# An FFN output gate: from the finished down sums (VectorE) into the down weights (GpSimd)

## Chip, cores and metric

The kernel runs on one NeuronCore of a Trainium2 chip. The metric is the device time of one execution in microseconds (us). The kernel before was run three times: 493.52, 494.44 and 493.52 us, median 493.52.

## What is computed

An adaptive-LayerNorm block over 2048 tokens of width 448, all in float32. A conditioning vector gives six rows of 448 (shift, scale and gate, for each of two sublayers). The second sublayer is a SwiGLU feed-forward network (FFN) of hidden width 1792, whose output is multiplied by its gate row `gb` before it is added to the residual:

```python
mod = (_silu(c) @ w_mod).reshape(c.shape[0], 6, 1, -1)
sa, ca, ga, sb, cb, gb = (mod[:, 0], mod[:, 1], mod[:, 2], mod[:, 3], mod[:, 4], mod[:, 5])
h = _layernorm(x, axis=-1) * (1 + ca) + sa
x = x + ga * _A_ref(h, ...)            # state-space convolution over the tokens
h = _layernorm(x, axis=-1) * (1 + cb) + sb
x = x + gb * ((_silu(h @ w_gate) * (h @ w_up)) @ w_down)
```

`gb` has one number for each of the 448 output columns, the same for all tokens. So `gb * (p @ w_down)` is also `p @ (w_down * gb)`, with the row multiplied into every row of `w_down`.

## The kernel before

**Tiling.** The tokens are 16 tiles of 128, taken in six blocks of 2, 2, 3, 3, 3, 3 tiles (`BLOCKS`). The hidden width is 14 steps of 128 (`NF`). For each block, `ffn` runs the 14 steps. In step f, `gate_up(f, nw)` makes both products of the block's tokens with weight tile f in two PSUM banks (L686), ScalarE takes the silu of one (L701), VectorE multiplies the other by it (L714). Then `down(f - 1)` adds the hidden part of the step before to the block's output sums, one PSUM bank `DN[q]` for each token tile (L730).

**Splits.** Matmuls run on a rounded type. To keep float32 precision each operand is split in a high part (a rounding copy) and a low part (the difference), and a product takes three matmuls: high by high, high by low, low by high. The hidden part is split by ScalarE (`phi`, L717) and VectorE (`plo`, L718). The weights are split once, in block 0: `split_w` for gate and up (ScalarE L120, VectorE L122 and L124) and `split_d` for down (ScalarE cast L112, VectorE subtraction L114). The split weights stay in SBUF for the later blocks.

**Order.** Nothing is scheduled for the kernel: instructions stand on each engine's queue in the order in which the code issues them. Ahead of the FFN the start-up works through a list of names (`PLAN`); in it `d00`, `d01`, `d10`, `d11` are the ScalarE and VectorE halves of the splits of down tiles 0 and 1. `eg` copies the finished row `gb` from PSUM to SBUF (L421), near the end of that list. The splits of down tiles 2 to 13 are at the head of `gate_up(f)` of block 0, that is ahead of that step's silu and product on the same engines.

**Loads.** SP's queue loads the weights. Raw down tiles rotate through three SBUF buffers (`rawd`): the load of tile f + 3 (L107) is issued in step f and waits until tile f has been split; it stands behind the load of gate-up tile f + 5 (L102), which waits for the split of tile f + 2.

**Other work in the steps.** `TIMES` places the norms and the convolution of the next block's tiles in the steps of this one (VectorE L148 to L186, L824 to L877; GpSimd L165 to L172 for the root of the variance; from block 1 on also GpSimd L824, L830, L843). `transposes` at the last step brings the next block's normalised rows into the layout `hhi`, `hlo` (TensorE L206, ScalarE L207 and L209, VectorE L211 and L212).

**End of a block.** For each token tile VectorE multiplies the down sum by `gb` into a spare SBUF buffer (L757), adds it to the residual `x` (L758), and SP stores the tile (L759). In the last block, tile 1's add is GpSimd's, and the last tile goes in two column parts, 256 and 192 wide (L753, L754), the first stored from ScalarE's queue and the second from SP's (L755).

Of the kernel before, what the change touches and what calls it, by code (L numbers as in the profile page):

```python
# [12 lines left out]
OP = mybir.AluOpType  # L13
# [3 lines left out]
L, D, N, F = 2048, 448, 256, 1792  # L17
# [4 lines left out]
NF = F // 128  # L22
# [18 lines left out]
ORDER = """sf x0 x1 sc m10 se m11 sd m20 m21 m00 sb m01 sa m40 m41 d0 w0 m30 m31 m50 w2 d1 x2 w1 x3 d2 m51"""  # L41

PLAN = """t1 t4 pa0 t2 pa1 pg0 pg1 t3 S1 ca h00 S2 ps0 wr wi ps1 a2 m0 t5 a3 sq1 k0 cb0 S3 ga cb1 w0 h01 gd h11 m1 k1 gm0 h10
hd0 sb0 gm1 hd1 gc1 v00 v10 gc0 o00 o01 sq0 o02 o10 v01 sa w02 d10 o13 st0 r0 o12 cbr v11 d11 o11 o14 sb1 n10 w2 w01
st1 r1 d00 sbr e0 n11 n20 du0 tr0 n21 hi0 du1 tr1 l0 fs l1 sbt lo00 hi1 w1 lo10 fl lo01 sbc x1 e1 lo11 w11 w21 x0 eg
w22 lc cbt w12 d01 cbc"""
EPS = 1e-5


# [3 lines left out]
def f32(ap):  # L53
    return ap.bitcast(F32)
# [3 lines left out]
def tile_kernel(ctx, tc, x, a_re, a_im, b_re, b_im, c_re, c_im, log_dt, dskip,  # L58
                wd, wgate_up, states, groups, vecs, dft, idft, out):
    nc = tc.nc  # L60
    sy, ve, sc, po, pe = nc.sync, nc.vector, nc.scalar, nc.gpsimd, nc.tensor
# [28 lines left out]
    wgu, raw, wdn, wp = {}, {}, {}, {}  # L90
# [5 lines left out]
    xn_of = [spare[2][:, 0:512], spare[2][:, 512:1024], spare[0][:, 0:512]]  # L96
# [9 lines left out]
        wp[j] = [pool.tile([128, D], F32R, name=f"wd{q}{j}") for q in "hl"]  # L106
        sy.dma_start(wdn[j], wd[j * 128:(j + 1) * 128, :])  # L107

    def split_d(j, part=None):
        hi, lo = wp[j]  # L110
        if not part:
            sc.copy(hi, wdn[j])  # L112
        if part != 0:
            ve.tensor_tensor(lo, wdn[j], f32(hi), op=OP.subtract)  # L114

    def split_w(j, part=None, en=ve):
        hi, lo, st = wgu[j][:, :, 0:3, :], wgu[j][:, :, 4:7, :], wgu[j][:, :, 3, :]
        w = raw[j]
        if not part:
            sc.copy(wgu[j][:, :, 0:4, :], w)  # L120
        if part is None or part == 1:
            en.tensor_tensor(lo, w[:, :, 0:3, :], f32(hi), op=OP.subtract)  # L122
        if part is None or part == 2:
            en.tensor_tensor(st[64:128], w[64:128, :, 3, :], f32(st[64:128]), op=OP.subtract)  # L124
# [16 lines left out]
    sbc = const.tile([128, 4], F32)  # L141
# [102 lines left out]
    with tc.tile_pool(name="pre", bufs=1) as pre:  # L244
# [54 lines left out]
        for z in range(2):  # L299
            e = slice(64 * z, 64 * z + 64)  # L300
# [110 lines left out]
        def flag_of():  # L411
# [10 lines left out]
        do = lambda g, *a: (lambda: g(*a))  # L422
# [35 lines left out]
            "w0": do(split_w, 0, 0), "w01": do(split_w, 0, 1, WV), "w02": do(split_w, 0, 2, WV),  # L458
            "w1": do(split_w, 1, 0), "w11": do(split_w, 1, 1), "w12": do(split_w, 1, 2),
            "w2": do(split_w, 2, 0), "w21": do(split_w, 2, 1), "w22": do(split_w, 2, 2),  # L460
            **{f"d{j}{z}": do(split_d, j, z) for j in range(2) for z in range(2)},
            "sq0": do(square, 0), "sq1": do(square, 1), "fs": flag_sum, "fl": flag_of,
        }
        names = PLAN.split()
# [197 lines left out]
    def run_blocks(pools, stages, first=None):  # L662
        work, hid = pools.work, pools.hid
        def ffn(ts, fresh, last, todo):
            n = len(ts) * 128
            dn, pp = [], {}
            qz = [(q, z) for z in range(3) for q in range(len(ts))]

            def gate_up(f, nw):
                head = fresh and f == 0  # L670
                if fresh and f > 1:
                    split_d(f)
                w = wgu[f]
                p = hid.tile([128, 256], F32, name="p") if fresh else p_of[f % 2]
                hi = hid.tile([128, MB * 128], F32R, name="phi")
                lo = hid.tile([128, MB * 128], F32R, name="plo")
# [39 lines left out]
                    split_w(nw, 1)  # L716
                sc.copy(hi[:, 0:n], ps[1][:, 0:n])  # L717
                ve.tensor_tensor(lo[:, 0:n], ps[1][:, 0:n], f32(hi[:, 0:n]), op=OP.subtract)  # L718
                if nw is not None:
                    split_w(nw, 2)  # L720

            def down(f, qz):
                if not dn:
                    dn.extend(DN[q] for q in range(len(ts)))
                hi, lo = pp[f]
                wh, wl = wp[f]
                for q, z in qz:
                    cs = slice(q * 128, (q + 1) * 128)
                    u, v = ((hi, wh), (hi, wl), (lo, wh))[z]
                    pe.matmul(dn[q][:, 0:D], u[:, cs], v, start=f == 0 and z == 0, stop=f == NF - 1 and z == 2)  # L730
# [12 lines left out]
                down(NF - 1, qz)  # L743
            m = len(ts) - 1
            for q, i in enumerate(ts):
                t = xn_of[q][:, 0:D]
                if last:
                    down(NF - 2, [(e, z) for e in ((0, 1) if q == 0 else range(q + 1, min(q + 2, m + 1))) for z in range(3)])
                    down(NF - 1, [(q, z) for z in range(3)])

                if last and q == m:
                    for a, e, dma in ((0, 256, sc), (256, D, sy)):
                        ve.tensor_tensor(dn[q][:, a:e], dn[q][:, a:e], gb[:, a:e], op=OP.mult)  # L753
                        ve.tensor_tensor(xs[i][:, a:e], dn[q][:, a:e], xs[i][:, a:e], op=OP.add)  # L754
                        dma.dma_start(out[i * 128:(i + 1) * 128, a:e], xs[i][:, a:e])  # L755
                    continue
                ve.tensor_tensor(t, dn[q][:, 0:D], gb, op=OP.mult)  # L757
                (po if last and q else ve).tensor_tensor(xs[i], xs[i], t, op=OP.add)  # L758
                sy.dma_start(out[i * 128:(i + 1) * 128, :], xs[i])  # L759

        for j in range(NP0, NP0 + NS):
            pools.load(j)
# [10 lines left out]
        for b, ts in enumerate(TILES):  # L773
            todo = {}
            if b + 1 < len(TILES):
# [208 lines left out]
```

## Time and profile before

| what | value |
|---|---|
| time of the three runs, median | 493.52 us (493.52 to 494.44) |
| profiled execution, span from first to last instruction | 491.7 us |
| mean granted TensorE clock in it | 0.995 |
| start-up until the first FFN matmul | 39.1 us |
| block 0 (L686, L730), to the first matmul of block 1 | 39.1 to 98.9 us |
| end of the last matmul | 484.06 us |
| last store issued | 486.32 us |
| splits of the down weights | 14 casts on ScalarE, median 570 ns; 14 subtractions on VectorE, median 624 ns |
| gate's multiplies on the down sums | 15 of 448 columns (median 616 ns), 2 parts of 256 and 192 |

The profile is of one further execution, whose own time is its span; the difference of 1.8 us to the runs' median lies outside its first and last instruction. In its rows, PE is TensorE, PEld its weight loads, DVE VectorE, ACT ScalarE, POOL GpSimd and SP SyncE; a q behind an engine is its instruction queue, where DMAs are issued. A timeline row is: start, length, engine, line, operation, written tile <- read tiles, shape, and in brackets the idle time ahead of it with what ended it. A row of one line's instructions gives the least, median and longest duration in ns. A row of a table by stretches gives, behind the length of the stretch, the busy time (and count) of PE, PEld, DVE, ACT and POOL, then granted clock, DMA share and GB/s. A row of DMA issues gives count, size and median us from issue to landing. In the chain of waits a row is start, length, and what the end of the program was waiting for then.

### The profile page before, as it was taken

The numbers are of one execution on the slowest core, as the hardware profiler recorded it, in microseconds if no ns is written. First come the engines' busy times: TensorE is split into PE (matmuls) and PEld (weight loads), VectorE is DVE, ScalarE is ACT, GpSimd is POOL, SyncE is SP. The second block draws the span as 40 slices with busy tenths as digits, with TensorE's granted clock in tenths as the row PEclk, the third lists the DMA queues.
The fourth block names the chain that finished last, engine by engine and source line by source line (L and its number), as shares of the span: only waits on it lengthen the run. The fifth ranks groups of instructions, "written<-read, shape, count | busy, mean of one in ns | idle before, by whom it ended". The sixth has DMA issues, their size and how long they took to land.

```text
span 491.7 us, 6939 instructions
## 1 busy us (share of the span) xinstructions
PE 482.0 (98%) x2759; PEld 452.5 (92%) x2759; DVE 265.9 (54%) x516; ACT 161.3 (33%) x348; POOL 70.3 (14%) x92
## 2 busy tenths in 40 slices
PE   8999999999999999999999999999999999999993
PEld 5659988999999999999999999999999999999992
DVE  4868999568886445634735553473465353221113
ACT  5665555622226112224412222521222161111110
POOL 2241001000010032411006140101541100000000
PEclk9999999999999999999999999999999999999998
DMA  8944752020000200000300000030000001000001
GB/s 309 404 165 159 232 188 86 15 95 1 0 3 21 75 1 0 2 1 2 98 15 1 2 0 2 2 112 1 0 2 1 1 0 57 0 1 0 1 0 64
DMA packets 11979, 26.04 MB, mean 53 GB/s; under 512 B 1825, under 2 KB 7842, under 8 KB 11938
## 3 DMA queue, kind: packets, MB, share of 16 engines
q1 hardware_dynamic: 11232, 25.33, 14.9%
q8 instruction: 23, 0.38, 0.3%
q10 hardware_dynamic: 706, 0.18, 0.2%
q14 instruction: 18, 0.15, 0.1%
HBM read 21.80 MB, written 3.67 MB: 52 GB/s over the span
## 4 chain that ended last, share of the span: by engine, by line
PE 97%; DVE 1%; ACT 0%; issue 0%; POOL 0%; POOLq 0%; DVEq 0%
PE bank L686 58%; PE dn L730 27%; PE bank L225 2%; PE bank L241 1%; PE bank L206 1%; PE dn L420 1%; PE bank L229 1%; PE cv L851 0%; PE cv L849 0%; PE bank L850 0%; PE cv L225 0%; PE bank L376 0%; PE bank L863 0%; PE cv L206 0%; PE cv L864 0%; PE dn L310 0%
## 5 line engine op out<-in xcount | busy, mean ns | idle before, releaser
L686 PE MATMUL bank<-hhi,gu 128*128 128x384 f32 (+1 forms) x1169 | 210.2, 319 | 0.0
L686 PEld LDWEIGHTS bank<-hhi,gu 128*128 128x128 f32 x1169 | 190.4, 188 | 3.1 <-issue 0.7
L686 PE MATMUL bank<-hlo,gu 128*128 128x384 f32 (+1 forms) x668 | 131.6, 319 | 0.0
L714 DVE TENSOR_TENSOR bank<-raw,bank 128x384 f32<-128x384 f32 (+1 forms) x69 | 36.9, 534 | 144.0 <-PE bank L686 128.6
L686 PEld LDWEIGHTS bank<-hlo,gu 128*128 128x128 f32 x668 | 109.7, 188 | 0.1
L717 ACT CAST phi<-bank 128x384 fp32r<-128x384 f32 (+1 forms) x83 | 36.8, 444 | 145.2 <-DVE bank L714 145.2
L701 ACT ACTIVATE raw<-bank 128x384 f32<-128x384 f32 (+1 forms) x70 | 32.8, 469 | 121.8 <-PE bank L686 115.4
L718 DVE TENSOR_TENSOR plo<-bank,phi 128x384 fp32r<-128x384 f32 (+1 forms) x83 | 42.5, 512 | 37.5 <-ACT phi L717 37.5
L730 PE MATMUL dn<-wdh,phi 128*128 128x448 f32 x224 | 60.4, 368 | 0.0
L730 PE MATMUL dn<-wdh,plo 128*128 128x448 f32 x224 | 60.2, 367 | 0.1
L730 PE MATMUL dn<-wdl,phi 128*128 128x448 f32 x224 | 59.9, 366 | 0.0
L730 PEld LDWEIGHTS dn<-wdh,plo 128*128 128x128 f32 x224 | 42.1, 188 | 3.9 <-DVE plo L710 0.4
L730 PEld LDWEIGHTS dn<-wdl,phi 128*128 128x128 f32 x224 | 42.1, 188 | 3.6
L730 PEld LDWEIGHTS dn<-wdh,phi 128*128 128x128 f32 x224 | 39.6, 188 | 1.7 <-ACT run L873 0.7
L824 POOL TENSOR_TENSOR m<-m,gm 128x448 f32<-128x448 f32 x9 | 11.1, 1237 | 64.9 <-DVE m L186 55.3
L165 POOL TENSOR_SCALAR rsb<-mvb 128x3 f32<-128x3 f32 (+2 forms) x7 | 1.9, 272 | 120.4 <-DVE mvb L149 120.4
L165 POOL TENSOR_SCALAR rsa<-mva 128x3 f32<-128x3 f32 (+1 forms) x6 | 1.4, 229 | 105.9 <-DVE mva L149 105.9
L120 ACT CAST gu<-raw 128x1024 fp32r<-128x1024 f32 x14 | 14.6, 1044 | 0.0
L758 POOL TENSOR_TENSOR x<-x,raw 128x448 f32<-128x448 f32 x1 | 1.1, 1129 | 91.2 <-DVE raw L757 91.2
L837 ACT CAST vh<-m 128x448 fp32r<-128x448 f32 x12 | 6.8, 567 | 22.3 <-DVE m L829 22.3
L830 POOL TENSOR_TENSOR v<-v,run 1x448 fp32r<-1x448 f32 x9 | 11.4, 1269 | 17.8 <-DMA run<-run 17.5
L225 PE MATMUL bank<-wm,cs 128*128 128x448 f32 x30 | 12.6, 550 | 0.0
(196 smaller groups left out, 426.8 us busy)
## 6 DMA issues: line engine op xcount, KB each, us to landing
raw<-in_B_w_gate_up_dram SPq DMA_DIRECT2D x14, 512.0 KB, 3.8
rawd<-in_B_w_down_dram SPq DMA_DIRECT2D x14, 224.0 KB, 3.9
x<-in_A_u_dram SPq DMA_DIRECT2D x12, 224.0 KB, 2.8
out_dram<-x SPq DMA_DIRECT2D x11, 224.0 KB, 1.9
wm<-in_w_mod_groups_dram SPq DMA_DIRECT2D x5, 448.0 KB, 8.1
wm<-in_w_mod_groups_dram SPq DMA_DIRECT2D x5, 336.0 KB, 7.9
rawd<-in_A_u_dram SPq DMA_DIRECT2D x4, 224.0 KB, 3.3
out_dram<-rawd SPq DMA_DIRECT2D x4, 224.0 KB, 1.9
```

Of the source, the lines that this page charges most:

```text
L120: sc.copy(wgu[j][:, :, 0:4, :], w)
L206: pe.transpose(ps[:, j * 128:(j + 1) * 128], xn[i][:, k * 128:(k + 1) * 128], ident)
L225: pe.matmul(ps[:, 0:D], cs[:, k:k + 1].to_broadcast([128, 128]), w[:, k * D:(k + 1) * D], start=k == 0, stop=False)
L686: pe.matmul(ps[s][:, 0:n], w[:, s, a], (hlo if lo else hhi)[:, k, 0:n], start=first and q == 0, stop=end and q == len(ka) - 1)
L701: sc.activation(p[:, 0:n], ps[0][:, 0:n], AF.Silu)
L714: ve.tensor_tensor(ps[1][:, 0:n], p[:, 0:n], ps[1][:, 0:n], op=OP.mult)
L717: sc.copy(hi[:, 0:n], ps[1][:, 0:n])
L718: ve.tensor_tensor(lo[:, 0:n], ps[1][:, 0:n], f32(hi[:, 0:n]), op=OP.subtract)
L730: pe.matmul(dn[q][:, 0:D], u[:, cs], v, start=f == 0 and z == 0, stop=f == NF - 1 and z == 2)
L824: (ve if on_v else po).tensor_tensor(v, h, g, op=OP.mult)
L830: (ve if on_v else po).tensor_tensor(v1[0:1], f32(v1[0:1]), run1[0:1], op=OP.add)
L837: sc.copy(vh, v0)
```

## The change

Each raw down tile is multiplied by `gb` on GpSimd, in place, before it is split (`gate_d`). The multiplies on the down sums go, and the residual add reads the PSUM sum directly. Since `gb` is not ready when the start-up list would split tiles 0 and 1, those four entries leave the list; their splits come in block 0, that of tile 0 behind the first step's hidden split, that of tile 1 at the head of step 1. Gates 0 and 1 are issued at the head of step 0, gate f + 1 at the head of step f. All adds at the block ends are VectorE's.

```diff
-hd0 sb0 gm1 hd1 gc1 v00 v10 gc0 o00 o01 sq0 o02 o10 v01 sa w02 d10 o13 st0 r0 o12 cbr v11 d11 o11 o14 sb1 n10 w2 w01
-st1 r1 d00 sbr e0 n11 n20 du0 tr0 n21 hi0 du1 tr1 l0 fs l1 sbt lo00 hi1 w1 lo10 fl lo01 sbc x1 e1 lo11 w11 w21 x0 eg
-w22 lc cbt w12 d01 cbc"""
+hd0 sb0 gm1 hd1 gc1 v00 v10 gc0 o00 o01 sq0 o02 o10 v01 sa w02 o13 st0 r0 o12 cbr v11 o11 o14 sb1 n10 w2 w01
+st1 r1 sbr e0 n11 n20 du0 tr0 n21 hi0 du1 tr1 l0 fs l1 sbt lo00 hi1 w1 lo10 fl lo01 sbc x1 e1 lo11 w11 w21 x0 eg
+w22 lc cbt w12 cbc"""
...
-    def split_d(j, part=None):
+    def gate_d(j):
+        po.tensor_tensor(wdn[j], wdn[j], gb, op=OP.mult)
+
+    def split_d(j):
         hi, lo = wp[j]
-        if not part:
-            sc.copy(hi, wdn[j])
-        if part != 0:
-            ve.tensor_tensor(lo, wdn[j], f32(hi), op=OP.subtract)
+        sc.copy(hi, wdn[j])
+        ve.tensor_tensor(lo, wdn[j], f32(hi), op=OP.subtract)
...
             def gate_up(f, nw):
                 head = fresh and f == 0
-                if fresh and f > 1:
+                if head:
+                    gate_d(0)
+                    gate_d(1)
+                elif fresh:
+                    if f + 1 < NF:
+                        gate_d(f + 1)
                     split_d(f)
...
                 ve.tensor_tensor(lo[:, 0:n], ps[1][:, 0:n], f32(hi[:, 0:n]), op=OP.subtract)
+                if head:
+                    split_d(0)
                 if nw is not None:
                     split_w(nw, 2)
...
-                if last and q == m:
-                    for a, e, dma in ((0, 256, sc), (256, D, sy)):
-                        ve.tensor_tensor(dn[q][:, a:e], dn[q][:, a:e], gb[:, a:e], op=OP.mult)
-                        ve.tensor_tensor(xs[i][:, a:e], dn[q][:, a:e], xs[i][:, a:e], op=OP.add)
-                        dma.dma_start(out[i * 128:(i + 1) * 128, a:e], xs[i][:, a:e])
-                    continue
-                ve.tensor_tensor(t, dn[q][:, 0:D], gb, op=OP.mult)
-                (po if last and q else ve).tensor_tensor(xs[i], xs[i], t, op=OP.add)
-                sy.dma_start(out[i * 128:(i + 1) * 128, :], xs[i])
+                for a, e, dma in ((0, 256, sc), (256, D, sy)) if last and q == m else ((0, D, sy),):
+                    ve.tensor_tensor(xs[i][:, a:e], dn[q][:, a:e], xs[i][:, a:e], op=OP.add)
+                    dma.dma_start(out[i * 128:(i + 1) * 128, a:e], xs[i][:, a:e])
```

More of the change, by code (lines that the diff above doesn't have):

```diff
@@ L460, in tile_kernel @@
             "w2": do(split_w, 2, 0), "w21": do(split_w, 2, 1), "w22": do(split_w, 2, 2),
-            **{f"d{j}{z}": do(split_d, j, z) for j in range(2) for z in range(2)},
             "sq0": do(square, 0), "sq1": do(square, 1), "fs": flag_sum, "fl": flag_of,
@@ L745, in ffn @@
             for q, i in enumerate(ts):
-                t = xn_of[q][:, 0:D]
                 if last:
```

## Prediction

> **What bounds the kernel now.** I read the page's head first, then its slices, then the chain of waits.
>
> ```profile
> span 491.7 us, 6939 instructions
> PE 482.0 (98%) x2759; PEld 452.5 (92%) x2759; DVE 265.9 (54%) x516; ACT 161.3 (33%) x348; POOL 70.3 (14%) x92
> ...
> DVE  4868999568886445634735553473465353221113
> ...
> PE 97%; DVE 1%; ACT 0%; issue 0%; POOL 0%; POOLq 0%; DVEq 0%
> ```
>
> TensorE is busy for 98% of the span and the chain lies on it for 97%. So work taken from or given to another engine counts in two places only: behind the last matmul, and where that engine comes so late that TensorE waits for it. VectorE is at half load on average, but in slices 4 to 7 (of 12.3 us each: 37 to 86 us, which is most of block 0) it stands at 8, 9, 9 and 9 tenths. The change takes work off VectorE everywhere and puts GpSimd work into just those slices. Both places need their own look.
>
> First the end of the chain of waits, then who sends the results out:
>
> ```profile
> 482.87 0.54 DVE raw L757
> 483.41 0.02 issue
> 483.43 0.62 DVE x L758
> 484.06 0.54 DVE raw L757
> 484.59 0.35 DVE dn L753
> ...
> 485.42 0.38 DVE dn L753
> ...
> 485.82 0.36 DVE x L754
> ```
> ```profile
> 483.10 0.37 PE L730 MATMUL dn<-wdh,plo 128*128 128x448 f32 x1
> ...
> 483.70 0.36 PE L730 MATMUL dn<-wdh,plo 128*128 128x448 f32 x1
> ```
> ```profile
> 484.08 2.14 SPq L759 DMA_DIRECT2D out_dram<-x  x2
> 486.32 0.40 SPq L755 DMA_DIRECT2D out_dram<-x  x1
> ```
> ```profile
> out_dram<-x SPq DMA_DIRECT2D x11, 224.0 KB, 1.9
> ...
> out_dram<-x SPq DMA_DIRECT2D x1, 96.0 KB, 3.4
> ```
>
> The last sum is there at 483.70 + 0.36 = 484.06. VectorE ends at 486.18 and the last store is issued at 486.32; it lands 3.4 us later, at 489.7, and the span closes at 491.7. VectorE bounds this tail: six operations stand in one queue, and half of them are the gate's.
>
> **The tail (removed).** After the change VectorE adds tile 0 (0.62) from 482.87 on, to 483.49. Tile 1's sum is complete at 483.10 + 0.37 = 483.47, so its add runs to 484.1 (it also replaces GpSimd's add on that tile). The two parts of tile 2 need 484.06 and follow at 484.1: 0.42 and 0.36, spaced as in the chain, end at 484.9. The last store is issued near 484.95 in place of 486.32: **-1.4 us**. Its 3.4 us to landing were in company, since the store of tile 1 and the other part of tile 2 go out within 1 us of it; four stores now stand as close, so I keep the 3.4. A lone store lands after 1.9; were that so here, 1.5 more would be won (-2.9). The stores are in all 672 KB; nothing else shares the queues then.
>
> **The middle block ends (removed).** Thirteen further multiplies of 0.62 us go from VectorE. TensorE is at 100% there and the chain never passes to VectorE, so I price them at nothing.
>
> **Start-up (removed, moved).** Splits of down tiles 0 and 1 (two ScalarE casts, two VectorE subtractions of 0.62) leave the written order. In the chain of the first 39 us none of them appears: nothing. They come back in block 0 behind the first gate-up:
>
> ```profile
> 38.93 0.53 ACT L421 COPY gb<-cv 128x448 f32<-128x448 f32 x1 [0.48 <-PE cv L229]
> ```
> ```profile
> 42.98 0.42 DVE L718 TENSOR_TENSOR plo<-bank,phi 128x256 fp32r<-128x256 f32 x1 [0.44 <-ACT phi L717]
> ```
> ```profile
> 44.72 0.57 PE L730 MATMUL dn<-wdl,phi 128*128 128x448 f32 x2
> ```
> ```profile
> 41.15 0.33 SPq L107 DMA_DIRECT2D rawd<-in_B_w_down_dram  x1
> ```
> ```profile
> rawd<-in_B_w_down_dram SPq DMA_DIRECT2D x14, 224.0 KB, 3.9
> ```
> ```profile
> 49.11 0.57 ACT L112 CAST wdh<-rawd 128x448 fp32r<-128x448 f32 x1
> ```
>
> The gate row is in SBUF at 39.46, so gates 0 and 1 can run from 39.5 to about 42, while ScalarE and VectorE wait for the first sums. The split of tile 0 then follows plo: subtraction from 43.4 to 44.05, needed at 44.72. Slack 0.65: no stall. On SP's queue the load of down tile 3 waits for that split (44.1 in place of 41.15), ahead of the load of gate-up tile 6. It lands 3.9 later, near 48.0; gate 3 follows, so its cast, at 49.11 before, has no cover left and goes as late as that gate does. With the two moved VectorE subtractions (some 0.6 each) block 0 starts with a lag of about 1.2 us.
>
> **Fourteen GpSimd multiplies (added), one per step of block 0.** Step f issues gate f+1, then a ScalarE cast that waits for gate f, with the silu of step f queued behind that cast, and VectorE's subtraction behind it, with the next hidden product. So a late gate holds up both engines. GpSimd itself is free. Its price lies here:
>
> ```profile
> 184.50 0.87 DVE L838 TENSOR_TENSOR vl<-m,vh 128x448 fp32r<-128x448 f32 x1 [0.63 <-ACT vh L837]
> ```
> ```profile
> 183.48 1.40 POOL L824 TENSOR_TENSOR m<-m,gm 128x448 f32<-128x448 f32 x1 [2.08 <-DVE m L186]
> 184.84 1.54 POOL L824 TENSOR_TENSOR v<-m,g 128x448 fp32r<-128x448 f32 x1
> ```
> ```profile
> L838 DVE TENSOR_TENSOR vl<-m,vh x12: 625/722/873, 118.1 to 379.4; 128x448 fp32r<-128x448 f32 x12
> ```
> ```profile
> L824 POOL TENSOR_TENSOR m<-m,gm x9: 1152/1157/1406, 177.9 to 363.3; 128x448 f32<-128x448 f32 x9
> ```
>
> A 448-wide GpSimd product takes 1.15 us by itself. Beside one VectorE operation that reads two SBUF tiles, that operation goes from 0.625 to 0.87 (+0.245), and the two products together lose 0.25 + 0.39 = 0.64. That is time-sharing: in 0.87 us VectorE did 0.625 of its work and GpSimd about 0.25 of its own. Against VectorE operations that read PSUM the products show no such loss (1.15 in most of the nine).
>
> The Trainium skill, in "GPSIMD Engine Reference", section "8. Key points", says the same as a rule: GpSimd shares its SBUF interfaces with VectorE and contends with VectorE instructions that have two SBUF inputs. The trace agrees with its 0.87 beside 0.625. By the rule this change sends GpSimd into the worst place; without it the sum would end with the tail.
>
> How much of block 0 is of that kind:
>
> ```profile
> 58.00:62.00 4.00, 4.00 (x32) 3.90 (x31) 3.90 (x8) 1.72 (x4) 0.00 (x0) 1.00 0.59 203
> 62.00:66.00 4.00, 4.00 (x32) 3.90 (x31) 3.94 (x8) 2.35 (x5) 0.00 (x0) 1.00 0.38 119
> 66.00:70.00 4.00, 4.00 (x22) 3.03 (x22) 3.88 (x9) 1.77 (x4) 0.00 (x0) 1.00 0.65 207
> ```
> ```profile
> 55.98 0.43 DVE L714 TENSOR_TENSOR bank<-p,bank 128x256 f32<-128x256 f32 x1 [0.84 <-PE bank L686]
> ...
> 62.35 0.42 DVE L718 TENSOR_TENSOR plo<-bank,phi 128x256 fp32r<-128x256 f32 x1
> ...
> 66.06 0.42 DVE L718 TENSOR_TENSOR plo<-bank,phi 128x256 fp32r<-128x256 f32 x1
> ```
> ```profile
> 64.13 0.57 PE L730 MATMUL dn<-wdh,plo 128*128 128x448 f32 x2
> ...
> 67.93 0.58 PE L730 MATMUL dn<-wdh,plo 128*128 128x448 f32 x2
> ```
>
> VectorE (fourth column after the stretch's length, PE and PEld) is busy for 3.9 of each 4 us from 58 to 70. A step is 67.93 - 64.13 = 3.80 us; of it only L714 and L718 (about 0.8 together) read PSUM, so some 3.0 of 3.8, 78%, read two SBUF tiles. A gate that must find 1.15 us there takes 0.78 x 1.15 = **0.9 us** from VectorE per step. The bounds: nothing (VectorE goes first and GpSimd alone lengthens), and 1.15 plus the cast's 0.57 that a stopped gate holds up (1.7).
>
> The lag of the first steps meets the 0.84 us idle ahead of 55.98 and is mostly used up there; I count none of it on. Behind that no idle is left. plo of step 6 ends at 66.48, its matmul starts at 67.93: cover of 1.45. Gates 4 to 7 run up to there: 4 x 0.9 = 3.6, less 1.45 = **+2.1 us** of TensorE waiting, by about 70 us. In step 7 the prefix matmuls give VectorE air, and I count nothing more until the block's end:
>
> ```profile
> 99.46 0.41 DVE L212 TENSOR_TENSOR hlo<-bank,hhi 128x256 fp32r<-128x256 f32 x1
> ```
> ```profile
> 98.88 0.98 PE L686 MATMUL bank<-hhi,gu 128*128 128x256 f32 x7
> 99.70 0.63 PE L686 MATMUL bank<-hlo,gu 128*128 128x256 f32 x4
> ```
>
> hlo of the last part is done at 99.87 and used by the fourth of the lower row's matmuls; seven took 99.70 - 98.88 = 0.82, so that is at 99.70 + 3 x 0.117 = 100.05: cover 0.18. Gates 12 and 13, late because the loads in front of them wait for late splits, take some 0.7 us out of the VectorE chain that ends there: **+0.5 us**. From block 1 on no gate runs.
>
> **Sum:** -1.4 + 2.1 + 0.5 = +1.2 us. It is a sum of differences inside the profiled span of 491.7; the runs' median lies 1.8 above it, which I take as unchanged: 493.52 + 1.2 = **494.7 us**, +0.24%. About 0.2%, 1.0 us, is what a measurement of this kernel can tell from no change.
>
> **Rivals.** *Gates hidden, tail gained.* If VectorE pays little per gate (each L838 met two products, so the 0.245 may belong to the handing over rather than to each operation; say 0.1 per gate), 4 x 0.1 stays under the cover of 1.45 and only the tail is left: 493.52 - 1.4 = 492.1, down to 490.6 if the last store also lands in 1.9. For it speaks GpSimd's 14% load and loads that land well before use; against it the sum 0.625 + 0.25 = 0.87, which is what sharing gives.
>
> *Gates run late without costing VectorE much.* ScalarE's cast then waits for a gate of 2 to 3 us, silu behind it, and part of the cover goes: a stall of about 1 us, 493.52 - 1.4 + 1.0 = 493.1.
>
> *Gates stopped by VectorE.* If a gate gets nothing while VectorE reads two tiles, a dense step is the two-tile work, then the gate, then the cast in turn: 3.0 + 1.15 + 0.57 = 4.7 in place of 3.8. Over some seven such steps that is 6.3 - 1.45 = 4.9 of stall: 493.52 - 1.4 + 4.9 = 497.0. It decides where a gate outlasts the 3.8 us step. L824's 1.54, not 2, speaks against it.
>
> For the tail the Trainium skill ("DMA: Bandwidth & Descriptors", section "Anatomy of one DMA — SWDGE (gpsimd) path") gives a fixed cost near 2.0 us per transfer and little for the bytes. By it the last store would land soon after 2 us, as the lone ones' 1.9 do and as the 3.4 of this trace doesn't; that is the lower end of the first rival.
>
> **Chances.** Forecast mechanism 0.50, with 493.6 to 495.7 as its own range and 0.12 of it below 494.5; gates hidden 0.27; late gates 0.13; stopped gates 0.10. Faster by over 0.2%: 0.27. Within: 0.13 + 0.12 = 0.25. Slower: 0.38 + 0.10 = 0.48. Range 491.5 to 497.0: it leaves out the better half of the first rival's extra landing gain and the worst of the last.
>
> **What would show it.** Right: the new GpSimd lines mean 2 to 3 us, not 1.15; L122's and L114's like in VectorE lengthen by 0.1 to 0.25 on the mean; TensorE idles in front of gate-up or down matmuls between 62 and 70 us, and block 1's first matmul moves from 98.9 to about 101.5; the distance from the last matmul to the last store's issue falls from 2.3 to about 0.9. Wrong: gates at 1.15 with TensorE unbroken through block 0 (then 492.1), a wait at the first down matmuls near 44.7 (the head's 0.65 of cover), or a tail that stays because the stores, not VectorE, end it.

## The result and the profile after

The changed kernel takes **495.77 us** (median of six runs, 495.41 to 497.43) against 493.9 for the kernel before (six runs, the three given above among them, 493.52 to 494.44). The measured ratio is 1.0048, 95% interval 1.0038 to 1.0058; the two medians alone give 1.0038. By either it is slower, from median to median by 1.9 us. Forecast were 494.7 and +1.2; the time lies inside the range of 491.5 to 497.0, and 0.07 above the 493.6 to 495.7 that the forecast mechanism had for itself.

The page of the changed kernel, with the lines that answer to those of before (line numbers move by up to seven):

```profile
span 493.7 us, 6933 instructions
PE 483.5 (98%) x2759; PEld 452.3 (92%) x2759; DVE 263.6 (53%) x500; ACT 160.7 (33%) x348; POOL 87.1 (18%) x105
...
DVE  4868999877885434644534553454555443122112
...
PE 81%; DVE 4%; issue 1%; DMA 1%; POOL 1%; ACT 1%; DVEq 0%; SPq 0%
```

The span has grown by 2.0. The chain of waits, which lay on TensorE for 97% of its length, now leaves it for VectorE, GpSimd, ScalarE and a load: somewhere TensorE waits for these. The total says little more. VectorE's busy time even fell, by 2.3: fifteen wide multiplies and two narrower ones went out of the block ends and one add came in, some 9.4 us less, while block 0 took 7.1 more.

**Where it went.** Cut the span at the first and the last FFN matmul (starts of the first L686 / L691 and the last L730 / L737):

| run | first | last | between | last to the span's end |
|---|---|---|---|---|
| before | 39.09 | 483.70 | 444.61 | 8.02 |
| after | 39.16 | 487.13 | 447.97 | 6.57 |

So the tail (the last column) gives 1.45 and the stretch of matmuls costs 3.36. All of the 3.36 lies in block 0 (59.79 to 62.66) and the first matmuls of block 1; blocks 2 to 5 take the same time in both, 83.0, 82.8, 82.8 and 79.8.

The tail, from VectorE's and TensorE's timeline, the list of transfers and SP's stores of the changed kernel (columns of the first two: start, length, engine and line; of the last: least, median and longest issue in ns):

```profile
486.21 2.01 DVE L758 TENSOR_TENSOR x<-dn,x 128x448 f32<-128x448 f32 x4
```
```profile
487.13 0.37 PE L737 MATMUL dn<-wdh,plo 128*128 128x448 f32 x1
```
```profile
out_dram<-x SPq DMA_DIRECT2D x1, 96.0 KB, 2.9
```
```profile
L759 SPq DMA_DIRECT2D out_dram<-x x12: 332/344/1044, 103.9 to 488.7; - x12
```

Four adds in a row, done at 488.22, 0.72 behind the end of the last matmul (487.50); before, VectorE ended 2.12 behind it. The last store is issued at 488.71, 1.58 behind that matmul's start, where it was 2.62, and lands 2.9 later, where it was 3.4. So the gain is 1.0 of issue and 0.5 of landing. The issue gains less than VectorE's 1.4, because SP's queue is still at the store ahead of it: that issue, from 487.57 on, is the longest of the row, 1.04 us, where its like took 0.33 before.

Now the loss. TensorE's timeline at the places where it falls behind, first before, then after; the bracket is idle time and what ended it:

```profile
48.93 0.58 PE L730 MATMUL dn<-wdh,plo 128*128 128x448 f32 x2
...
63.31 0.58 PE L730 MATMUL dn<-wdh,phi 128*128 128x448 f32 x2
...
67.11 0.58 PE L730 MATMUL dn<-wdh,phi 128*128 128x448 f32 x2
...
92.59 0.58 PE L730 MATMUL dn<-wdh,plo 128*128 128x448 f32 x2
...
100.17 0.86 PE L686 MATMUL bank<-hhi,gu 128*128 128x256 f32 x6
```
```profile
49.22 0.68 PE L737 MATMUL dn<-wdh,plo 128*128 128x448 f32 x2
...
65.33 0.67 PE L737 MATMUL dn<-wdh,phi 128*128 128x448 f32 x2 [1.49 <-ACT phi L722]
...
69.56 0.67 PE L737 MATMUL dn<-wdh,phi 128*128 128x448 f32 x2 [0.18 <-ACT phi L722]
...
95.44 0.67 PE L737 MATMUL dn<-wdh,plo 128*128 128x448 f32 x2 [0.15 <-DVE plo L723]
...
103.58 0.98 PE L691 MATMUL bank<-hhi,gu 128*128 128x256 f32 x7
```

Each row of after minus its row of before, less the 0.07 by which the FFN starts later, is the lag at that point: 0.2, 1.95, 2.4, 2.8, 3.3. Most of it arises in one wait of 1.49 for a hidden product near 65 us; 0.9 comes at the end of the block. TensorE's wait names ScalarE, but ScalarE's cast itself waited for VectorE's product. VectorE over block 0, grouped by line and shape, before and then after (busy us and mean ns of one stand behind the bar):

```profile
L122 DVE TENSOR_TENSOR gu<-raw,gu 128x768 fp32r<-128x768 f32 x12 | 11.4, 950 | 0.0
L114 DVE TENSOR_TENSOR wdl<-rawd,wdh 128x448 fp32r<-128x448 f32 x13 | 8.1, 621 | 1.4 <-ACT wdh L112 1.3
L714 DVE TENSOR_TENSOR bank<-p,bank 128x256 f32<-128x256 f32 x14 | 5.9, 425 | 5.6 <-PE bank L686 2.8 <-ACT gu L120 1.5 <-ACT p L701 1.4
...
L124 DVE TENSOR_TENSOR gu<-raw,gu 64x256 fp32r<-64x256 f32 x13 | 5.4, 423 | 0.4
...
L824 DVE TENSOR_TENSOR m<-m,gm 128x448 f32<-128x448 f32 x2 | 1.3, 626 | 0.1
```
```profile
L123 DVE TENSOR_TENSOR gu<-raw,gu 128x768 fp32r<-128x768 f32 x12 | 14.1, 1174 | 0.3 <-ACT gu L121 0.3
L115 DVE TENSOR_TENSOR wdl<-rawd,wdh 128x448 fp32r<-128x448 f32 x14 | 9.2, 654 | 1.9 <-ACT wdh L114 1.7
L125 DVE TENSOR_TENSOR gu<-raw,gu 64x256 fp32r<-64x256 f32 x13 | 8.9, 689 | 0.4
L719 DVE TENSOR_TENSOR bank<-p,bank 128x256 f32<-128x256 f32 x14 | 5.9, 422 | 1.1 <-ACT p L706 1.1
...
L824 DVE TENSOR_TENSOR m<-m,gm 128x448 f32<-128x448 f32 x2 | 2.1, 1044 | 0.1
```

The operations that read two SBUF tiles have grown, by 0.03 to 0.42 us on the mean; the product that reads PSUM (L714, now L719) has not. And VectorE's idle time ahead of that product, 5.6 us before, is down to 1.1: that was the cover. A mean hides the kind of growth. VectorE's timeline, and then GpSimd's, of after:

```profile
47.00 1.83 DVE L123 TENSOR_TENSOR gu<-raw,gu 128x768 fp32r<-128x768 f32 x1
...
58.37 1.37 DVE L123 TENSOR_TENSOR gu<-raw,gu 128x768 fp32r<-128x768 f32 x1 [0.25 <-ACT gu L121]
...
62.00 1.46 DVE L824 TENSOR_TENSOR m<-m,gm 128x448 f32<-128x448 f32 x1
...
64.78 0.94 DVE L123 TENSOR_TENSOR gu<-raw,gu 128x768 fp32r<-128x768 f32 x1
```
```profile
46.86 1.15 POOL L110 TENSOR_TENSOR rawd<-rawd,gb 128x448 f32<-128x448 f32 x1 [3.61 <-DMA rawd<-in_B_w_down_dram]
...
57.77 1.15 POOL L110 TENSOR_TENSOR rawd<-rawd,gb 128x448 f32<-128x448 f32 x1 [1.25 <-DMA rawd<-in_B_w_down_dram]
...
61.52 1.46 POOL L110 TENSOR_TENSOR rawd<-rawd,gb 128x448 f32<-128x448 f32 x1 [2.59 <-DMA rawd<-in_B_w_down_dram]
64.97 1.79 POOL L110 TENSOR_TENSOR rawd<-rawd,gb 128x448 f32<-128x448 f32 x1 [1.99 <-DMA rawd<-in_B_w_down_dram]
```

Lay the two on each other. GpSimd starts at 46.86 and takes its ordinary 1.15, to 48.01; L123 starts at 47.00 and takes 1.83 in place of 0.95, that is 0.88 more, and the product had 1.01 left to run. At 58.37 the product has 0.55 left and L123 takes 0.42 more. At 64.78 L123 is first and takes its 0.94; the product that starts at 64.97 takes 1.79, 0.64 more. Nothing is shared in proportion: whoever starts first keeps its own speed, and the other is held nearly until it ends. That is the theory which the runs below test: **exclusion for a whole instruction**. Its rival is the prediction's time-sharing; two more rivals are that the waits for late products, or the changed order of the splits, do the harm.

GpSimd's products over all of after (minimum, median, maximum ns):

```profile
L110 POOL TENSOR_TENSOR rawd<-rawd,gb x14: 1149/1204/1787, 39.7 to 92.7; 128x448 f32<-128x448 f32 x14
```

### The profile page after: what moved, and what is told of

Same layout as the page of the kernel before. It is cut to its first block, busy times and chain, and to the rows that moved or that the text cites. A ratio compares the mean times of both kernels' runs of the same rounds, so it can differ in the third digit from the quotient of the medians.

```text
span 493.7 us, 6933 instructions
## 1 busy us (share of the span) xinstructions
PE 483.5 (98%) x2759; PEld 452.3 (92%) x2759; DVE 263.6 (53%) x500; ACT 160.7 (33%) x348; POOL 87.1 (18%) x105
## 4 chain that ended last, share of the span: by engine, by line
PE 81%; DVE 4%; issue 1%; DMA 1%; POOL 1%; ACT 1%; DVEq 0%; SPq 0%
PE bank L691 53%; PE dn L737 25%; DMA rawd<-in_B_w_down_dram 1%; PE bank L207 1%; DVE gu L123 1%; PE cv L851 0%; PE cv L849 0%; PE bank L850 0%; POOL rawd L110 0%; DVE wdl L115 0%; PE cv L207 0%; DVE plo L723 0%; DVE bank L719 0%; DVE gu L125 0%; DVE v L824 0%
## 5 line engine op out<-in xcount | busy, mean ns | idle before, releaser
L691 PE MATMUL bank<-hhi,gu 128*128 128x384 f32 (+1 forms) x1169 | 210.2, 318 | 0.0
L691 PEld LDWEIGHTS bank<-hhi,gu 128*128 128x128 f32 x1169 | 190.4, 188 | 3.1 <-issue 0.7
L691 PE MATMUL bank<-hlo,gu 128*128 128x384 f32 (+1 forms) x668 | 132.0, 319 | 0.0
L719 DVE TENSOR_TENSOR bank<-raw,bank 128x384 f32<-128x384 f32 (+1 forms) x69 | 36.9, 535 | 153.8 <-PE bank L691 138.9
L691 PEld LDWEIGHTS bank<-hlo,gu 128*128 128x128 f32 x668 | 109.8, 188 | 0.5 <-DVE hlo L213 0.3
L737 PE MATMUL dn<-wdh,phi 128*128 128x448 f32 x224 | 60.6, 369 | 1.7 <-ACT phi L722 1.7
L737 PE MATMUL dn<-wdh,plo 128*128 128x448 f32 x224 | 60.3, 368 | 0.3 <-DVE plo L723 0.2
L737 PE MATMUL dn<-wdl,phi 128*128 128x448 f32 x224 | 59.9, 366 | 0.0
L737 PEld LDWEIGHTS dn<-wdh,plo 128*128 128x128 f32 x224 | 41.8, 188 | 5.0 <-DVE plo L723 0.9
L737 PEld LDWEIGHTS dn<-wdl,phi 128*128 128x128 f32 x224 | 42.1, 188 | 3.6
L737 PEld LDWEIGHTS dn<-wdh,phi 128*128 128x128 f32 x224 | 39.6, 188 | 3.8 <-ACT phi L722 2.7
L110 POOL TENSOR_TENSOR rawd<-rawd,gb 128x448 f32<-128x448 f32 x14 | 18.2, 1310 | 32.2 <-DMA rawd<-in_B_w_down_dram 24.1
L123 DVE TENSOR_TENSOR gu<-raw,gu 128x768 fp32r<-128x768 f32 x13 | 14.9, 1155 | 0.3 <-ACT gu L121 0.3
## 6 DMA issues: line engine op xcount, KB each, us to landing
wm<-in_w_mod_groups_dram SPq DMA_DIRECT2D x5, 448.0 KB, 8.2
```

The costliest lines, as they stand in the source:

```text
L110: po.tensor_tensor(wdn[j], wdn[j], gb, op=OP.mult)
L691: pe.matmul(ps[s][:, 0:n], w[:, s, a], (hlo if lo else hhi)[:, k, 0:n], start=first and q == 0, stop=end and q == len(ka) - 1)
L719: ve.tensor_tensor(ps[1][:, 0:n], p[:, 0:n], ps[1][:, 0:n], op=OP.mult)
```

## The experiments

Ratios are to the kernel before, run in turn on the same chip (its median there 493.35 to 493.65). "Stretch" is the first FFN matmul to the last, 444.61 before and 447.97 after.

**1. No product at all, and a narrow one.** Two edits of after:

```diff
 def gate_d(j):
-    po.tensor_tensor(wdn[j], wdn[j], gb, op=OP.mult)
+    pass                                                                        # e1
+    po.tensor_tensor(wdn[j][:, 0:16], wdn[j][:, 0:16], gb[:, 0:16], op=OP.mult) # e2
```

> This kernel leaves the gate out of the result: it is the changed kernel without its fourteen GpSimd products, with the moved splits, the loads' order and the short tail kept. Theory P (a GpSimd product and a VectorE operation that reads two SBUF tiles run one at a time, and this costs TensorE 3.4 us in block 0): the stall is gone and the tail's 1.4 us stay, 493.9 - 1.4 = 492.5. Rival W (the gate's place between load and cast makes loads and casts late, whatever it costs on the port): also 492.5. Rival M (the splits of tiles 0 and 1, moved into block 0, crowd VectorE): most of the stall stays, 494.5 to 495.8.

Measured: 492.0 (491.43 to 492.45), ratio 0.997 (0.9958 to 0.9982); stretch 444.63, from its last matmul to the span's end 6.26.

> The GpSimd products cover 16 of the 448 columns (the other columns stay without gate), so every wait and every place in the queues is that of the changed kernel while a product lasts some 0.2 to 0.3 us in place of 1.15. P: hardly any hold, 492.5 to 493.1. W: loads, products and casts still stand in line, so 494.5 or more. M: 494.5 or more.

Measured: 492.23 (491.65 to 492.8), 0.9977 (0.9968 to 0.9986); stretch 444.69; products of 0.23 us. W and M both wanted 494.5 or more here. So the new order, the moved splits, the waits between GpSimd, ScalarE and the loads cost nothing by themselves, and the shorter tail is worth 1.1 to 1.4 us in the medians of these two. The whole loss needs products of full width.

With e1 as the measure, the holds in block 0 of after can be counted. Eleven of its VectorE operations are longer than their kind in e1, by 0.42 to 0.99, and no other by more than 0.01. Each of the eleven has two SBUF inputs and starts while a product runs, one for each of eleven products. Of the other three products one meets no start of a VectorE operation, and two meet only operations that read PSUM.

**2. Full products that nobody reads.** Before, with GpSimd at work beside it:

```diff
+def gate_d(j):
+    po.tensor_tensor(ga, wdn[j], gb, op=OP.mult)     # ga is read no more here
 ...
+    if fresh and f + 1 < NF:
+        gate_d(f + 1)
```

> The kernel before with thirteen GpSimd products (tiles 1 to 13 by the gate row) into a buffer that nobody reads, at the places of the changed kernel; gate, splits and tail as before. P: VectorE and the products hold each other as in the changed kernel, without its waits: TensorE loses 1.5 to 3.4 us, 495.4 to 497.3. W and M: nothing waits for the products and no split moves, 493.9.

Measured: 494.99 (494.72 to 495.92), 1.0035 (1.0021 to 1.0049); stretch 446.46, +1.85. No wait, no moved split, no change of the computation: the mere presence of the products costs 1.85 us of the stretch.

**3. The same products on VectorE.** After, with `ve.` in place of `po.` in `gate_d`.

> The same products on VectorE: no second engine on the port, but 0.55 us more on VectorE per step. P: four of them ahead of step 6 are 2.2 us on a cover of 1.45, so 0.8 us of stall, some more at the block's end, 493.0 to 494.0, under the changed kernel's 495.8. W: the product still stands between load and cast, but no longer waits in a queue of its own, 494 to 496.

Measured: 495.32 (494.14 to 496.57), 1.0034 (1.0022 to 1.0045); stretch 447.80. P's expectation was missed by more than 1 us; W's, 494 to 496, was met, though W had fallen with the narrow products of run 1. VectorE's busy time in block 0 speaks for load and not for order. These are the stretches of block 0 of four kernels; behind the stretch's length stand TensorE, its weight loads, VectorE, ScalarE and GpSimd; first before, then e1, after and e4:

```profile
39.09:98.88 59.79, 59.79 (x417) 55.02 (x416) 49.78 (x97) 33.23 (x67) 3.30 (x6) 1.00 0.43 139
```
```profile
39.76:99.59 59.83, 59.83 (x418) 54.99 (x417) 50.23 (x98) 34.01 (x69) 2.94 (x6) 1.00 0.41 139
```
```profile
39.16:101.82 62.66, 60.81 (x417) 54.91 (x416) 56.86 (x97) 32.98 (x68) 21.53 (x20) 1.00 0.41 133
```
```profile
40.21:102.80 62.59, 60.77 (x417) 55.00 (x416) 57.05 (x111) 32.86 (x68) 3.67 (x6) 1.00 0.39 133
```

Fourteen products on VectorE itself add 57.05 - 50.23 = 6.8 us to its busy time, 0.49 each, near the 0.55 expected; what was too small was the stall priced for them. On GpSimd they add 56.86 - 50.23 = 6.6. Handing them over relieved VectorE of next to nothing.

**4. After, with products that nobody reads or waits for.** `gate_d` writes to `ga`, the gate is left out, everything else stays as in after.

> The changed kernel with its fourteen products written to a buffer that nobody reads, so casts and subtractions don't wait for them (the gate is left out of the result); moved splits and short tail stay. The FFN's stretch from its first to its last matmul was 444.6 us before, 448.0 with the change, 446.5 with idle products in the kernel before. If the wait of the casts for held and late gates makes the remaining 1.5 us: 446.5 here and 494.0 less the tail, about 493.4 to 494.2. If the moved splits make it, because they meet the holds: 448.0 and 495.3 to 495.8.

Measured: 495.69 (495.33 to 496.81), 1.0048 (1.0035 to 1.0061); stretch 447.82. After has 447.97: ScalarE's waits for late products cost about 0.15. But this is 1.36 more than run 2, with the tail won. Either the moved splits or the two first products make that difference; run 8 tells them apart.

**5. Each product in two, and in four pieces.**

```diff
 def gate_d(j):
-    po.tensor_tensor(wdn[j], wdn[j], gb, op=OP.mult)
+    for e in (slice(0, D // 2), slice(D // 2, D)):                # e9: four of D // 4
+        po.tensor_tensor(wdn[j][:, e], wdn[j][:, e], gb[:, e], op=OP.mult)
```

> Each product is made as two of 224 columns. If two operations exclude each other for their whole length (a VectorE operation that finds a product running is held until that product ends), no VectorE operation of block 0 is lengthened by more than about 0.65 us, where the changed kernel has up to 0.96, and GpSimd's second half queues behind VectorE instead: FFN stretch between 446.5 and 449. If the port is shared in time in proportion, the lengthening by product stays as it is and so does the stretch, 448.0.

Measured: 493.66 (492.56 to 494.04), 1.0001 (0.9992 to 1.001); stretch 446.29, just under the range expected under exclusion, where sharing wanted 448.0. Half of the loss is gone. The most that one VectorE operation of block 0 gains over its kind in e1 is 0.52, where it was 0.99 with whole products.

> After, with each GpSimd product written as four of 112 columns. The narrow products (16 columns) took 0.22 and the whole ones 1.15, so a quarter should take near 0.45 and VectorE be held for at most that each time. If the hold is for the length of the one GpSimd instruction that came first, no VectorE operation of 448 columns takes above 0.62 + 0.45 = 1.1, but four products together are some 1.8 of GpSimd time in place of 1.15, so that more VectorE operations meet one: the stretch from first to last FFN matmul at 445.5 to 446.3 (halves 446.3, none 444.6) and 493.0 to 493.7. If what counts is the sum of GpSimd's time beside VectorE, it is worse than whole products: above 448.0 and 495.8.

Measured: 494.4 (493.6 to 495.39), 1.0017 (1.0008 to 1.0026); stretch 446.93: between the two expectations, and met by neither. Block 0 of the halves, then of the quarters:

```profile
39.65:100.82 61.17, 60.34 (x417) 55.01 (x416) 54.05 (x98) 33.23 (x68) 26.65 (x34) 1.00 0.41 136
```
```profile
39.02:100.69 61.67, 60.35 (x418) 55.02 (x417) 53.18 (x97) 32.92 (x68) 35.62 (x62) 1.00 0.41 135
```

VectorE's extra time over e1 falls with the pieces, 6.6, 3.8, 3.0, while GpSimd's busy time rises, 21.5, 26.7, 35.6. With exclusion a shorter instruction holds VectorE for less: with quarters the longest gain of one operation is 0.27. But four pieces lose again a part of what two had gained, and the waits of ScalarE's cast for GpSimd rise, from 3.9 us with halves to

```profile
ACT wdh L115 <- POOL rawd L111: 5.4, 3, 2.6
```

with quarters. That late products are what turns the gain back is read from this row alone; it was not tried apart, and run 4 had priced the 3.8 us of such waits in after at only 0.15 of the stretch.

**6. The port by itself.** The theory still rested on overlaps found in a crowded stretch. So an idle test was set into block 5 of before, where both engines have room:

```diff
+def probe(kind, hi, lo, ps):             # steps 1-3, 4-6, 7-9, 10-12 of block 5
+    if kind < 3:
+        po.tensor_tensor(ga[:, 0:384], gb[:, 0:384], f32(lo[:, 0:384]), op=OP.mult)
+        for k in range(14):              # 64 columns each
+            ve.tensor_tensor(t[:, o], gb[:, o], gb[:, o], ...)    # kind 0: two in SBUF
+            ve.tensor_tensor(t[:, o], ps[:, ...], gb[:, o], ...)  # kind 1: one in PSUM
+            ve.tensor_copy(t[:, o], gb[:, o])                     # kind 2: one, in SBUF
+    else: seven GpSimd products of 48 columns beside three of 448 on VectorE
```

> Before, with an idle test in the last block, where VectorE and GpSimd have room; nobody reads what it writes. Behind the hidden product of steps 1 to 12 GpSimd gets one product of 384 columns (it waits for that step's plo; some 1.0 by itself, from the 1.15 of 448) and VectorE, at the same time, fourteen narrow operations of 64 columns one behind the other: in steps 1 to 3 with two SBUF tiles as inputs, in steps 4 to 6 with one of the inputs in PSUM, in steps 7 to 9 copies with one SBUF input. In steps 10 to 12 GpSimd gets seven narrow products of 48 columns and VectorE three of 448 with two SBUF inputs. Whole-instruction exclusion (my theory) expects of steps 1 to 3 that one narrow VectorE operation takes as long as the rest of GpSimd's product, near 1.0, or the product as long as a VectorE operation in front of it more, and that the others take what they take alone; of steps 4 to 6 that none is long; of steps 10 to 12 that a narrow product is stretched to what is left of a VectorE operation, up to 0.6, or a VectorE operation by one narrow product, some 0.3. Time-sharing (the prediction's reading) expects the narrow operations that run beside the product all to be longer by some 40%, and none near 1.0; the product then takes 1.4 or more. Of steps 7 to 9 neither says anything.

Measured (one run, 494.45; minimum, median, maximum ns of one): the three kinds of narrow VectorE operation, the narrow GpSimd products and the wide VectorE operations beside them, and the wide GpSimd products:

```profile
L675 DVE TENSOR_TENSOR raw<-gb x42: 207/211/1055, 414.3 to 428.4; 128x64 f32<-128x64 f32 x42
...
L677 DVE TENSOR_TENSOR raw<-bank,gb x42: 212/215/217, 431.4 to 444.5; 128x64 f32<-128x64 f32 x42
...
L679 DVE COPY raw<-gb x42: 180/184/1019, 448.5 to 462.0; 128x64 f32<-128x64 f32 x42
...
L667 POOL TENSOR_TENSOR ga<-gb,plo x21: 277/286/700, 465.8 to 479.7; 128x48 f32<-128x48 f32 x21
...
L669 DVE TENSOR_TENSOR raw<-gb x9: 615/625/627, 465.5 to 478.2; 128x448 f32<-128x448 f32 x9
...
L671 POOL TENSOR_TENSOR ga<-gb,plo x9: 1007/1019/1058, 414.5 to 460.1; 128x384 f32<-128x384 f32 x9
```

In each of steps 1 to 3 exactly one of fourteen narrow operations is long, 1.04 to 1.055, and the other thirteen take the 0.21 that they take alone. Time-sharing would have made several of them longer by some 40% each. GpSimd's product is hardly longer for it, 1.01 to 1.06 in all nine steps, where sharing wanted 1.4. VectorE's PSUM readers are not held at all (217 is the longest). The other way round, a GpSimd product of 0.28 takes up to 0.70 behind a VectorE operation of 0.62, which itself loses nothing. And the copies, with one SBUF input, are held as well, one of fourteen, for 1.01: the theory had said nothing of those.

The Trainium skill says this in "SBUF — State Buffer", section "SBUF: two separate sides": the port pair of VectorE and GpSimd is a lock and no split of bandwidth; of a GpSimd operation and a VectorE one with two SBUF inputs or in a two-port mode, the first has it for its whole instruction, and the other is blocked. The 1.055 in place of 0.21 agrees. The prediction had drawn on another page and read the kind of contention from one pair of rows.

**7. The gate elsewhere.** If it is VectorE's fullness that makes the holds cost, the products should be free where VectorE is not full. Before, with the raw down tiles loaded a second time, gated and split again into the same weight tiles late in the kernel, so that only the last block uses gated weights; blocks 0 to 4 keep their multiplies, and the last block ends as in after.

```diff
+def regate(j):
+    hi, lo = wp[j]
+    t = g_of[j % 2]
+    po.tensor_tensor(t, t, gb, op=OP.mult)
+    sc.copy(hi, t)
+    ve.tensor_tensor(lo, t, f32(hi), op=OP.subtract)
 ...
+    if b == len(TILES) - 2:                       # e7: one tile per step of block 4
+        load_g(f)
+        if f > 1: regate(f - 2)
+    if last:                                      # e8 instead: tile f + 1 in step f of block 5
+        for j in (0, 1) if f == 0 else (f + 1,):
+            if j < NF: regate(j)
+            if j + 2 < NF: load_g(j + 2)
```

> Meant to have the gain without the loss: block 0 and the sums of blocks 0 to 4 as before; during block 4, where VectorE is half idle, the raw down tiles are loaded again, multiplied by the gate row on GpSimd and split anew, so only the last block works with gated weights and adds its sums directly. If holds cost only where VectorE has no slack: FFN stretch 444.6, tail 1.4 us shorter, 492.0 to 492.6. If holds cost anywhere: 493 or more.

Measured: 496.56 (494.27 to 497.68), 1.0059 (1.0044 to 1.0073). The profile is of the fastest of the six executions, 494.27; in it block 4 took 85.21 in place of 82.85. Four executions took 496.38 to 497.68, at a granted clock of 0.993 or 0.994 where the two fastest had 0.997 and 0.998, and no profile shows what they add. The expectation was missed: VectorE is busy for only half of block 4 (41.18 of 82.85 before), but the convolution's products of the next block stand in order on GpSimd's queue, and so do the casts on ScalarE's. ScalarE's and TensorE's waits in block 4 (the first was 5.5 before, the others were not there):

```profile
ACT vh L853 <- DVE m L845: 7.9, 3, 2.9
ACT wdh L124 <- POOL raw L123: 3.0, 2, 1.8
```
```profile
PE cv L865 <- ACT vh L853: 1.5, 1, 1.5
```

Nearly all of the loss arises at that one convolution matmul, at 370.65. Ahead of it VectorE's subtraction for a split (L125) waited 1.85 for its cast and took 1.02 in place of 0.62, and the addition whose result `vh` copies (L845) took 1.55 in place of 0.60. So late gates and holds both stand in the chain; the run doesn't tell their shares, and a VectorE with room on average was not enough.

> Before, block 0 untouched (raw gates nowhere), and the gate moved to the last block only: two raw down tiles are loaded again in the last steps of block 4, and in step f of block 5 GpSimd multiplies the gate's row into raw tile f+1 (tiles 0 and 1 in step 0), ScalarE and VectorE split it again into the same weight tiles, and the load of tile f+3 is issued behind. Blocks 0 to 4 keep the multiply of the finished sums; the last block's closing adds are those of after. Block 5 has no convolution of a next block in it: GpSimd is empty there and VectorE a third busy. If the loss of after comes from GpSimd products standing in front of a VectorE that is full (my theory), block 5's TensorE keeps its 79.8 us, the stretch from first to last FFN matmul its 444.6, and the 1.4 of the tail are won: 492.0 to 492.6. If a GpSimd product beside VectorE costs TensorE wherever it stands (the rival), 14 products cost 1.9 or more as in the idle-product run: block 5 near 81.7 and 494 to 495.

Measured: **492.57** (491.56 to 494.01), 0.998 (0.997 to 0.9991); stretch 444.62, tail 6.76. Block 5, which has no convolution in it, first before and then e8:

```profile
403.87:483.70 79.83, 79.76 (x434) 77.36 (x433) 20.94 (x41) 13.93 (x30) 0.00 (x0) 1.00 0.03 9
```
```profile
404.07:483.94 79.87, 79.79 (x435) 77.35 (x433) 28.46 (x55) 20.46 (x44) 14.19 (x12) 1.00 0.15 44
```

With twelve of the products in it, and fourteen more splits on VectorE and ScalarE, TensorE's block is as long as it was. This version beats both kernels: the tail is won and the stretch pays nothing for it. But no VectorE operation was held here. The subtractions have their ordinary length (behind the bar busy us and mean ns):

```profile
L125 DVE TENSOR_TENSOR wdl<-rawd,wdh 128x448 fp32r<-128x448 f32 x7 | 4.3, 619 | 1.2 <-ACT wdh L124 1.2
```

One product met one of them and was itself the one held (1.47); the others met only operations that read PSUM, or none. So the run shows that products which hold nothing cost nothing. Holds where there is room are shown by the idle test of run 6: six of 0.84 fell into its block 5, which took 79.91 in place of 79.83.

**8. Moved splits, or first products?** Run 2 with all fourteen products (splits of tiles 0 and 1 still in the start-up), and run 4 without the first two (splits moved, twelve products, gate left out):

```diff
+    if head:                 # e11, on run 2's kernel
+        gate_d(0)
 ...
-    if head:                 # e12, on run 4's kernel
-        gate_d(0)
-        gate_d(1)
```

> The idle-product run (before, with GpSimd products that nobody reads) with all fourteen products, the first two at the first gate-up as in after. The splits of down tiles 0 and 1 stay in the start-up. Thirteen products cost the stretch of FFN matmuls 1.85 us; fourteen with the splits moved into block 0 cost 3.2. If the moved splits make the difference, this run stays near 446.5 (+1.9) and 495.0. If it is the fourteenth product, which stands in front of the start-up's last splits at 39.7, it comes to 447.8 (+3.2) and 495.7 less the tail's 1.4 not won, that is near 497.

Measured: 495.26 (495.01 to 496.23), 1.0042 (1.0026 to 1.0059); stretch 446.48, +1.87.

> The unread-product run (after, with products that nobody reads and nobody waits for; the gate is left out) without the products of tiles 0 and 1: twelve are left, from step 1 on, and the splits of tiles 0 and 1 stay moved into block 0. If the moved splits make the difference between +1.85 and +3.2, it is still there: 447.5 or more, 495.4. If the first products make it, which hold VectorE at 39.7 to 42, the stretch falls to some 446.4 (+1.8) and the time to 494.0.

Measured: 495.25 (494.73 to 495.9), 1.0036 (1.0024 to 1.0049); stretch 447.47, +2.86. So the table of the stretch reads:

| | no full products | full products |
|---|---|---|
| splits of tiles 0, 1 in the start-up | 444.61 | +1.85 (13), +1.87 (14) |
| splits moved into block 0 | +0.02 | +2.86 (12), +3.21 (14, unread), +3.36 (after) |

The moved splits alone cost nothing, the products alone 1.85; together they cost 1.0 to 1.3 more than that. That the splits use up idle time of VectorE which would have covered the holds fits its queue, but the runs show only the sum.

## Why the prediction was right or wrong

- **What bounds the kernel, and where to look** (the tail, and block 0 with a full VectorE): right. Nothing else moved; the "middle block ends" were worth nothing, as said, and so was the start-up (first FFN matmul 39.09, then 39.16; over all profiles 38.8 to 39.9 with the old list and 38.9 to 40.2 with the new one, so that a difference of some tenths could not be seen).
- **The tail, -1.4:** measured -1.45 in the profiles. VectorE's share was right, 2.12 to 0.72 behind the last matmul (its queue held seven operations, four of them the gate's, not six and three). That the total was right too is luck: the last store no longer follows VectorE at once but waits for SP's issue of 1.04, which takes 0.35 off the gain, and a landing of 2.9 in place of 3.4 makes up for it. The prediction had named such a tail as a sign of being wrong, but priced no issue on SP's queue; in e1 and e8 that issue took 1.37 and 1.50, and the last store landed 2.3 and 2.4 after its own. Why the issue is long is not shown. A single profile tells the tail no better than to some 0.7: it is 5.97 to 6.76 in the other runs that end like after, and 7.32 in e3, which ends like before (8.02). The section of the Trainium skill that the prediction cites for the tail ("DMA: Bandwidth & Descriptors", "Anatomy of one DMA — SWDGE (gpsimd) path") is about transfers issued from GpSimd; these stores leave SP's and ScalarE's queues, and the last three landed after 2.4 to 3.8.
- **The head's slack of 0.65:** right, no wait at the first down matmul. The first lag is 0.2 at 49.22, one matmul group later.
- **Contention with VectorE operations on two SBUF tiles:** right as the cause, shown by runs 1, 2 and 6.
- **"That is time-sharing":** wrong. It was read from one pair, 0.625 to 0.87 and 1.15 to 1.54, in which two GpSimd products stood one behind the other, so that a hold of 0.25 looked like a slower rate. From it came the "2 to 3 us" per product; measured are 1.31 on the mean, 1.15 to 1.79. Excluding is milder for GpSimd and, where it strikes, harsher for one VectorE operation.
- **"0.9 us per step":** too much. By run 1, after's products add 6.6 / 14 = 0.47 each to VectorE. A hold costs 0.4 to 1.0, one for each of eleven products; the three that met no operation on two SBUF tiles made none.
- **The lag of the moved splits, "I count none of it on":** wrong, and it made good for the step above. Run 8 prices it at 1.0 to 1.3 in company with the products, over the whole stretch. The +2.1 by about 70 us stands against a measured lag of 2.4: a nearly right term by luck, from two errors against each other.
- **The end of block 0, +0.5:** right for what it priced. The lag is 2.87 at block 1's first matmul (98.88, then 101.82) and 3.34 at 103.58, behind the matmuls that use `hlo`: 0.47. What the sum lacks is the 0.4 ahead of that, from 2.46 to 2.87, at the matmul that waits for `plo` at 95.44: for the steps behind step 7 the prediction had counted nothing "until the block's end".
- **The rivals.** "Gates hidden" fell by run 2, "late gates" by run 4 (0.15 us). "Stopped gates" had the right kind of contention with the wrong loser: it let only GpSimd be stopped, by a VectorE that always comes first, and put 4.9 of stall on it.
- **The sum:** +1.2 forecast, +1.9 measured: 0.3 from the lag by 70 us, 0.4 from the uncounted wait for `plo`. The other 0.4 of the miss of 1.07 us is the base, 493.52 in three runs and 493.9 in six.

## What to carry to other kernels

Work that is handed from VectorE to GpSimd may relieve it of nothing where VectorE is full of operations on two SBUF operands: here 14 products cost VectorE 6.6 us from GpSimd's queue and 6.8 on its own. Before moving work, look for the stretch in which the engines that it touches, and the queues that it stands on, have room: products and their splits cost TensorE 3.4 us in block 0, 2.4 in block 4 and nothing in block 5, where they held no VectorE operation. An engine's mean load does not settle this: in block 4 VectorE was half idle. Price two edits that lean on the same idle time together: alone the moved splits cost nothing, beside the products 1.0 or more.

## What the runs showed of the hardware

- A VectorE operation with two SBUF inputs that starts behind a GpSimd product is held nearly until that ends (64 columns: 0.21 to 1.055; 768 columns: 0.95 to 1.83), and the other way round (48 columns on GpSimd: 0.28 to 0.70). Reading one operand from PSUM avoids it (0.217 at most). A plain float32 copy from SBUF to SBUF does not (0.18 to 1.02).
- Of seven narrow GpSimd products beside three wide VectorE operations, three were stretched (0.53 to 0.70), one for each of these, and the VectorE operations stayed at 0.615 to 0.627.
- Pieces have a price on GpSimd: products of 448 columns take 1.15, of 384 columns 1.01, of 48 columns 0.28 and of 16 columns 0.23.
